# Tap products that write PSUM channel by channel, and copies out of PSUM that write SBUF at a step

## The chip, the cores and the metric

The kernel runs on one core of one Trainium2 chip. The metric is the time of one execution on the device in microseconds (us). TensorE is called PE, VectorE DVE, ScalarE ACT, GpSimd POOL; SP is the engine from whose queue most transfers are issued. A tile of PSUM holds 128 partitions; PSUM has eight banks of 512 fp32 numbers per partition, and the kernel hands them out as eight slots.

## The reference, cut to what matters

Two layers in a row over 2048 positions and 512 channels: a state-space convolution with a residual, and an MLP with a residual. The change lies in the making of the convolution kernel `K`, one row of 2048 taps for each of the 512 channels `d`, summed over 128 states `n`:

```python
dt = jnp.exp(log_dt)[:, None]
A = A_re + 1j * A_im
logdA = dt * A
dB = dt * Bc
P = jnp.exp(logdA[:, :, None] * l[None, None, :])
K = jnp.einsum("dn,dnl,dn->dl", Cc, P, dB).real
...
Yf = Uf * Kf[None, :, :, :]
y = irfft2(Yf)[..., :L] + u * Dskip
h = x + y
h2 = h + (gelu(layernorm(layernorm(h)) @ w1 + b1) @ w2 + b2)
```

## The kernel before, in words

**Stages.** The start loads the inputs and tables and prepares angles and magnitudes. Then exponentials and sines are made for the factors of `P` (up to about 105 us), with the first layer norm and the transform of the input between them. The taps are summed from the factors, transformed (`kspec`, `kspec1`, `fstage`), multiplied with the transform of the input (line 1203), transformed back (line 1213), and from about 145 us on the MLP runs (lines 1330 to 1348), with the second half of the convolution in between.

**The tap products.** A power of the state's factor is split in two: 20 offsets (the list `ROWS`, `NA` = 20) times 33 multiples of eight (`NB` = 33, from -16 to 16). For each channel the kernel holds a table of 128 states by 20 offsets and one of 128 states by 33 multiples, each as a real and an imaginary part: `EA`, `IA` and `EB`, `IB`. In SBUF the 128 channels of a group lie side by side within each offset, so one channel's 20 or 33 columns are 128 bf16 numbers (256 bytes) apart. A channel needs two matmuls, both over 128 states: real times real (line 1058) and imaginary times imaginary (line 1059), added up in PSUM. The weights are 128 by 20, the moving operand 128 by 33. There are four groups of 128 channels (`kgen(c)`, c = 0 to 3, called at lines 1373 and 1379), so 512 + 512 matmuls. Four channels, `g` = 0 to 3, go to the four column tiles of PE, each with its own 32 partitions of PSUM.

**The PSUM tile and the copy.** Within a group of 128 channels `i` counts the 32 channels of one column tile. They are filled in two tiles (`KIS`): one of two banks with 11 channels each, and one of a bank with 10. In a bank the sum for multiple `k` of channel `i` stands at place `k * n + i`, with `n` = 11 or 10: the channels are neighbours, and one matmul writes its 33 sums `n` numbers apart. When a tile is full, `evac` (lines 575 to 587) copies it to SBUF as bf16, on ACT (line 578) or DVE (line 580) as the written order says: 2 x 33 x 11 = 726 numbers a partition, or 33 x 10 = 330. In SBUF the place of a sum is `k` first and then the channel: `Kg` (groups 0 and 1 interleaved, 64 numbers from one `k` to the next) or `kgc` (groups 2 and 3, 32 numbers from one `k` to the next). So a copy writes runs of 11 or 10 neighbours, 128 or 64 bytes apart. Both copies of a group are followed by an addition on DVE at line 1072 (the skip term `Dz`), and then by the products that read the taps: line 1088 in `kspec` for groups 0 and 1, line 1113 in `kspec1` for groups 2 and 3, and line 1134 in `ktail`.

**Order.** The order of all operations is written out by hand in the list `ORDER`, which also says which of two engines takes a copy; the string `SLOTS` says which bank each PSUM tile gets. Each engine works through its own part in that order. The costs handed to `add` play no part at run time.

Of the kernel before, what the change touches and what calls it, by code (L numbers as in the profile page):

```python
# [25 lines left out]
NA = len(ROWS)  # L26
NB = 33
# [283 lines left out]
class Sched:  # L311
# [10 lines left out]
    def add(self, eng, cost, fn, r=(), w=(), new=(), lat=0.0, pr=None, byts=0, soft=(), softw=(), hv=None):  # L322
        o = Op()
        o.soft = sorted({self.wr[k] for x in soft for k in self.keys(x) if k in self.wr} | {i for x in softw for k in self.keys(x) for i in self.rd.get(k, ())})
        o.eng = eng if isinstance(eng, tuple) else (eng,)
        o.cost = cost if isinstance(cost, tuple) else (cost,)
        o.fn, o.lat, o.i, o.new, o.byts = fn, lat, len(self.ops), tuple(new), byts
        o.ni, o.act, o.st, o.md = 0, 0.0, 0.0, []
        o.hv = int(o.eng[0] == "DVE") if hv is None else hv
        o.pr = self.pr if pr is None else pr  # L330
        o.key = "%g%s" % (o.pr, o.eng[0][0])
        deps = set()
        for x in r:
            for k in self.keys(x):
                p = self.wr.get(k)
                if p is not None:
                    deps.add(p)
        for x in w:
            for k in self.keys(x):
                p = self.wr.get(k)  # L340
                if p is not None:
                    deps.add(p)
                deps.update(self.rd.get(k, ()))
        for x in r:
            for k in self.keys(x):
                self.rd.setdefault(k, []).append(o.i)
        for x in w:
            for k in self.keys(x):
                self.wr[k] = o.i
                self.rd[k] = []  # L350
        o.deps = sorted(deps)
        o.ps = [x for x in list(r) + list(w) if isinstance(x, Ps)]
        self.ops.append(o)
        return o
# [47 lines left out]
def c_dve(n, mode=1, psum=False):  # L402
    return (0.08 if n < 64 else 0.065) + n / mode / 960.0
# [3 lines left out]
def kernel(ctx, tc, A_u, A_A_re, A_A_im, A_B_re, A_B_im, A_C_re, A_C_im, A_log_dt, A_Dskip,  # L407
# [4 lines left out]
    class Pe:  # L412
        n, dry, act, st, md = 0, True, 0.0, 0.0, []
# [30 lines left out]
    def pst(p, dt=f32):  # L444
        a = banks[:, 512 * p.slot:512 * (p.slot + p.n)]
        return a if dt == f32 else a.bitcast(dt)
# [128 lines left out]
    def evac(out_fn, in_fn, n, r, w, pr=None, only=None):  # L575
        def fn(e):
            if e == "ACT":
                act.copy(out_fn(), in_fn())  # L578
            else:
                dve.tensor_copy(out_fn(), in_fn())  # L580
        if only == "ACT":
            add("ACT", c_act(n), fn, r=r, w=w, pr=pr)
        elif only == "DVE":
            add("DVE", c_dve(n, 1, True), fn, r=r, w=w, pr=pr, hv=0)
        else:
            add(("ACT", "DVE"), (c_act(n), c_dve(n, 1, True)), fn, r=r, w=w, pr=pr)
# [455 lines left out]
    def kgen(c, pr):  # L1042
        Ar, Br, Ai, Bi = EA[c], EB[c], IA[c], IB[c]
        kg = Kg[0] if c < 2 else kgc[c - 2]
        ks = (lambda: kg.ap()[:, :, c]) if c < 2 else kg.ap
        for grp in KIS:
            S.pr = pr + 0.01 * KIS.index(grp)
            p = Ps(n=len(grp))

            first = True  # L1050
            for nb, (i0, n) in enumerate(grp):
                for lo, hi in ((0, n // 2), (n // 2, n)):
                    def fn(e, p=p, nb=nb, i0=i0, n=n, lo=lo, hi=hi):
                        for i in range(lo, hi):
                            for g in range(4):
                                d = 32 * g + i0 + i
                                o = pst(p)[32 * g:32 * g + NA, 512 * nb:512 * nb + NB * n].rearrange("p (k i) -> p k i", i=n)[:, :, i]
                                pe.matmul(o, lhsT=Ar.ap()[:, :, d], rhs=Br.ap()[:, :, d], start=True, stop=False, tile_position=(0, 32 * g))  # L1058
                                pe.matmul(o, lhsT=Ai.ap()[:, :, d], rhs=Bi.ap()[:, :, d], start=False, stop=True, tile_position=(0, 32 * g))  # L1059
                    add("PE", 0.1376 * (hi - lo), fn, r=[Ar, Br, Ai, Bi], w=[p], new=[p] if first else [])  # L1060
                    first = False
            i0, n = grp[0]
            N = len(grp)

            def ofn(i0=i0, n=n, N=N):
                a = ks()[:, :, i0:i0 + n * N]
                return a.rearrange("p k (b i) -> p b k i", b=N)

            def ifn(p=p, n=n, N=N):
                return pst(p).rearrange("p (b q) -> p b q", b=N)[:, :, 0:NB * n].rearrange("p b (k i) -> p b k i", i=n)  # L1070
            evac(ofn, ifn, NB * n * N, [p], [kg])
        add("DVE", c_dve(32), lambda e: dve.tensor_tensor(ks()[:, 0], ks()[:, 0], Dz.ap()[:, c, :], ALU.add), r=[kg, Dz], w=[kg])

# [391 lines left out]
```

## Time and profile before

| | |
|---|---|
| median of 3 runs | 237.22 us (236.57 to 238.54) |
| the profiled execution, its own time | 235.58 us |
| its span, first to last instruction | 233.8 us |
| mean granted PE clock | 0.967 |
| PE busy | 204.2 us (87%) |
| DVE busy | 172.9 us (74%) |
| ACT busy | 158.6 us (68%) |
| lines 1058 and 1059 | 1024 matmuls between 58.0 and 104.9 us |
| copies out of the tap tiles | six on ACT, two on DVE, at 63, 71, 73, 74, 94, 94, 104 and 105 us |

How to read the lines that follow: a row of a group gives line, engine and operation, then what is written and read, partitions by elements, the count, the busy time in us, the mean duration of one in ns, and after the second bar the idle time of the engine before them with what ended it. `ar` is the one large SBUF tile in which everything lies, `ps` is PSUM, and `128*20 128x33` is a matmul with a weight of 128 by 20 and a moving operand of 128 by 33. PEld is the load of weights. A row in order of time gives the start in us, the duration in us, engine, line, operation and count. A row of the chain gives start and duration of one piece of the work that ended last. A row for one line gives durations as smallest, median and largest. Matmuls overlap one another, so their pace is seen in the distance of their starts.

### The profile page before, as it was taken

Reading aid. Unit: us, or ns where it says so; the run is one execution under the profiler, and the core shown is the slowest. Engines: PE = TensorE matmul, PEld = TensorE weight load, DVE = VectorE, ACT = ScalarE, POOL = GpSimd, SP = SyncE. Lnnn points to the kernel's source line nnn. Section 1 sums busy time; section 2 is a strip of 40 time slices with the busy share of each in tenths; the row PEclk is TensorE's granted clock in tenths of the full one; section 3 lists DMA queues with packets and bytes.
Section 4 is the critical chain, followed back from the end, with each engine's and each line's share of the span. In section 5 each row is a group of like instructions: output and inputs, shape, how many; then the busy total and the mean of one; then the engine's idle time right before and its main releaser. Section 6 shows DMA issues by size and latency. Waiting matters only on the chain.

```text
span 233.8 us, 8092 instructions
## 1 busy us (share of the span) xinstructions
PE 204.2 (87%) x3608; PEld 117.0 (50%) x3616; DVE 172.9 (74%) x282; ACT 158.6 (68%) x194; POOL 13.4 (6%) x23
## 2 busy tenths in 40 slices
PE   7318878888998996999999968999999999999992
PEld 4305633335675455677567555654444344444551
DVE  2999999999979765659799999989955993010222
ACT  4999999999986893756898479685155308405500
POOL 3000300000160000000000010100000110000000
PEclk9965999999999998899999999999999999999998
DMA  5998263270000363346989966530333045002212
GB/s 157 185 172 138 62 185 95 60 254 13 6 6 3 98 159 138 99 105 195 221 141 230 311 159 161 137 90 12 81 77 91 5 100 126 20 0 59 56 40 61
DMA packets 43160, 25.18 MB, mean 108 GB/s; under 512 B 30195, under 2 KB 40693, under 8 KB 43126
## 3 DMA queue, kind: packets, MB, share of 16 engines
q1 hardware_dynamic: 42142, 23.67, 41.9%
q10 hardware_dynamic: 984, 1.00, 1.4%
q8 instruction: 28, 0.46, 0.8%
q14 instruction: 6, 0.05, 0.1%
HBM read 14.14 MB, written 5.28 MB: 83 GB/s over the span
## 4 chain that ended last, share of the span: by engine, by line
PE 51%; DVE 15%; DMA 11%; ACT 11%; issue 5%; SPq 3%; POOL 2%; DVEq 0%; ACTq 0%
PE ps L1330 16%; PE ps L1346 16%; DMA ar<-in_A_u_dram 5%; ACT ar L578 4%; PE ps L1213 4%; ACT ar L1030 3%; SPq L594 3%; ACT ar L992 3%; PE ps L1058 3%; DVE ar L874 3%; DVE ar L1203 2%; PE ps L918 2%; PE ps L1028 2%; PE ps L1059 2%; DVE ar L922 2%
## 5 line engine op out<-in xcount | busy, mean ns | idle before, releaser
L578 ACT CAST ar<-ps 128x1024 bf16<-128x1024 f32 (+4 forms) x64 | 56.8, 940 | 14.9 <-PE ps L1213 4.1
L1332 ACT ACTIVATE ar<-ps,ar 128x512 bf16<-128x512 f32 (+1 forms) x44 | 27.8, 685 | 36.3 <-PE ps L1330 25.7
L1330 PE MATMUL ps<-ar 128*128 128x512 bf16 (+1 forms) x176 | 41.1, 379 | 0.0
L1346 PE MATMUL ps<-ar 128*128 128x512 bf16 (+2 forms) x180 | 40.2, 366 | 0.7 <-DVE ar L1290 0.2
L1348 DVE TENSOR_TENSOR ar<-ps,ar 128x512 bf16<-128x512 f32 (+1 forms) x17 | 10.7, 656 | 31.8 <-PE ps L1346 25.1
L580 DVE CAST ar<-ps 128x1024 bf16<-128x1024 f32 (+3 forms) x22 | 21.5, 988 | 9.6 <-PE ps L1059 2.9
L1346 PEld LDWEIGHTS <-ar 128*128 128x128 bf16 (+1 forms) x187 | 18.0, 98 | 20.1 <-issue 1.2
L1330 PEld LDWEIGHTS <-ar 128*128 128x128 bf16 (+1 forms) x176 | 17.2, 100 | 20.1 <-DMA ar<-in_B_w_dram 0.2
L1203 DVE TENSOR_TENSOR ar<-ar 128x2048 bf16<-128x2048 bf16 x20 | 23.8, 1218 | 0.6 <-PE ps L1213 0.5
L1030 ACT ACTIVATE ar<-ps 128x1024 bf16<-128x1024 int16 x20 | 19.9, 1039 | 5.0 <-PE ps L1028 4.4
L1213 PE MATMUL ps<-ar 64*128 64x128 bf16 x672 | 21.4, 216 | 1.7 <-DVE ar L1203 1.2
L1213 PEld LDWEIGHTS <-ar 64*128 64x128 bf16 x672 | 18.8, 94 | 6.2 <-issue 2.9
L1058 PE MATMUL ps<-ar 128*20 128x33 bf16 x512 | 20.1, 249 | 0.7 <-issue 0.7
L1059 PE MATMUL ps<-ar 128*20 128x33 bf16 x512 | 20.0, 247 | 0.0
L1058 PEld LDWEIGHTS <-ar 128*20 128x20 bf16 x512 | 16.8, 124 | 4.5 <-issue 4.1
L649 POOL TENSOR_TENSOR ar<-ar 128x4 f32<-128x4 f32 (+1 forms) x6 | 10.3, 1716 | 137.2 <-DVE ar L654 129.9
L897 PE MATMUL ps<-ar 128*32 128x512 bf16 x256 | 16.5, 381 | 1.5 <-ACT ar L957 1.2
L1059 PEld LDWEIGHTS <-ar 128*20 128x20 bf16 x512 | 17.3, 127 | 0.8 <-issue 0.4
L1028 PE MATMUL ps<-ar 128*32 128x256 f16 (+2 forms) x288 | 13.4, 289 | 3.6 <-issue 1.8
L992 ACT ACTIVATE ar<-ps 128x1024 bf16<-128x1024 int16 x16 | 15.8, 1050 | 0.8 <-PE ps L984 0.7
L744 ACT ACTIVATE ar<-ar 128x1024 bf16<-128x1024 f32 x16 | 15.6, 1047 | 0.6 <-DVE ar L1247 0.6
L918 PE MATMUL ps<-ar 128*64 128x512 bf16 (+2 forms) x160 | 14.7, 303 | 0.3 <-ACT ar L578 0.2
(87 smaller groups left out, 258.9 us busy)
## 6 DMA issues: line engine op xcount, KB each, us to landing
ar<-in_A_u_dram SPq DMA_DIRECT2D x16, 128.0 KB, 6.2
out_dram<-ar SPq DMA_DIRECT2D x30, 64.0 KB, 2.0
ar<-in_A_u_dram SPq DMA_DIRECT2D x7, 256.0 KB
ar<-in_B_w_dram SPq DMA_DIRECT2D x2, 640.0 KB, 6.2
ar<-in_B_w_dram SPq DMA_DIRECT2D x3, 344.0 KB, 7.6
AK_d<-ar SPq DMA_DIRECT2D x2, 512.0 KB, 4.2
ar<-AK_d SPq DMA_DIRECT2D x2, 512.0 KB
AKc_d<-ar SPq DMA_DIRECT2D x4, 256.0 KB, 4.5
```

The source lines that it names most:

```text
L578: act.copy(out_fn(), in_fn())
L580: dve.tensor_copy(out_fn(), in_fn())
L918: pe.matmul(pst(p)[64 * h:64 * h + 64, w * (k + r):w * (k + r) + w], lhsT=T.ap()[:, f, r, :], rhs=v[f:f + 1].ap()[:, 0, :], start=True, st ...
L992: add("ACT", c_act(1024), lambda e, p=p, sc=sc, cs=cs: act.activation(sc[cs].ap().rearrange("p c e d -> p e c d"), pst(p, i16).rearrange(" ...
L1030: add("ACT", c_act(1024), lambda e, sc=sc: act.activation(sc.ap().rearrange("p z a b -> p (z a b)"), pst(p, i16).rearrange("p (n two) -> p ...
L1058: pe.matmul(o, lhsT=Ar.ap()[:, :, d], rhs=Br.ap()[:, :, d], start=True, stop=False, tile_position=(0, 32 * g))
L1059: pe.matmul(o, lhsT=Ai.ap()[:, :, d], rhs=Bi.ap()[:, :, d], start=False, stop=True, tile_position=(0, 32 * g))
L1203: dve.tensor_tensor(pq.ap().rearrange("p n d -> p (n d)"), a, b_, ALU.mult)
L1213: pe.matmul(pst(p)[:, 512 * h + 128 * k:512 * h + 128 * k + 128], lhsT=q.ap()[rows, x, :], rhs=TP[w].ap()[rows, f0 // 2 + k, :], start=(n ...
L1330: pe.matmul(pst(p)[:fs], lhsT=w1s[dc].ap()[:, fc * P:fc * P + fs], rhs=ybuf.ap().rearrange("p (t c) k -> p c t k", c=4)[:, dc], start=(dc ...
L1332: add("ACT", c_act(512, 1), lambda e, p=p, fc=fc, fs=fs: act.activation(hT.ap()[:fs, fc, :], pst(p)[:fs], ACT.Gelu_apprx_tanh, bias=b1_sb. ...
L1346: pe.matmul(pst(p)[:, c0:c1], lhsT=hT.ap()[:fs, fc, 128 * t:128 * t + 128], rhs=w2s[fc].ap()[:fs, c0:c1], start=(fc == 0), stop=(fc == NFC ...
```

## The change

In the PSUM tile the two indices change places: the sum for multiple `k` of channel `i` now stands at `i * 33 + k`, so that a matmul writes 33 neighbours. The copy reads the tile in that order, straight through as before, and its output runs over `k` fastest: each bf16 number is written 64 numbers (`Kg`) or 32 numbers (`kgc`) after the one before. What lies where in SBUF after the copy is the same in both kernels. Numbers of instructions, engines, order, slots and transfers do not change.

```diff
                             for g in range(4):
                                 d = 32 * g + i0 + i
-                                o = pst(p)[32 * g:32 * g + NA, 512 * nb:512 * nb + NB * n].rearrange("p (k i) -> p k i", i=n)[:, :, i]
+                                o = pst(p)[32 * g:32 * g + NA, 512 * nb:512 * nb + NB * n].rearrange("p (i k) -> p i k", k=NB)[:, i, :]
                                 pe.matmul(o, lhsT=Ar.ap()[:, :, d], rhs=Br.ap()[:, :, d], start=True, stop=False, tile_position=(0, 32 * g))
                                 pe.matmul(o, lhsT=Ai.ap()[:, :, d], rhs=Bi.ap()[:, :, d], start=False, stop=True, tile_position=(0, 32 * g))
...
             def ofn(i0=i0, n=n, N=N):
                 a = ks()[:, :, i0:i0 + n * N]
-                return a.rearrange("p k (b i) -> p b k i", b=N)
+                return a.rearrange("p k (b i) -> p b i k", b=N)
 
             def ifn(p=p, n=n, N=N):
-                return pst(p).rearrange("p (b q) -> p b q", b=N)[:, :, 0:NB * n].rearrange("p b (k i) -> p b k i", i=n)
+                return pst(p).rearrange("p (b q) -> p b q", b=N)[:, :, 0:NB * n].rearrange("p b (i k) -> p b i k", k=NB)
             evac(ofn, ifn, NB * n * N, [p], [kg])
```

## The prediction

> **What bounds the kernel now.** I read the page first, then the groups by shape, then the order of time around the two places that the diff touches. On the page I took the busy shares, the slices, the chain's shares by line and the groups of the tap products:
>
> ```profile
> span 233.8 us, 8092 instructions
> PE 204.2 (87%) x3608; PEld 117.0 (50%) x3616; DVE 172.9 (74%) x282; ACT 158.6 (68%) x194; POOL 13.4 (6%) x23
> PE   7318878888998996999999968999999999999992
> ACT  4999999999986893756898479685155308405500
> PE ps L1330 16%; PE ps L1346 16%; DMA ar<-in_A_u_dram 5%; ACT ar L578 4%; PE ps L1213 4%; ACT ar L1030 3%; SPq L594 3%; ACT ar L992 3%; PE ps L1058 3%; DVE ar L874 3%; DVE ar L1203 2%; PE ps L918 2%; PE ps L1028 2%; PE ps L1059 2%; DVE ar L922 2%
> L1058 PE MATMUL ps<-ar 128*20 128x33 bf16 x512 | 20.1, 249 | 0.7 <-issue 0.7
> L1059 PE MATMUL ps<-ar 128*20 128x33 bf16 x512 | 20.0, 247 | 0.0
> ```
>
> PE is the engine that is nearly always busy, and it holds most of the chain that ended last. The two lines of tap products, 1058 and 1059, hold 3% and 2% of that chain, between 58 and 105 us. So there are two ways for this change to matter: through the pace of these 1024 matmuls, and through the eight copies out of their PSUM tiles.
>
> **The tap products.** Nothing is added or removed: still 512 + 512 matmuls, the same operands, the same order. Only the step of the PSUM writes goes from 11 (or 10) fp32 numbers to 1. What is this worth? Matmuls are pipelined, so I go by the starts and not by the means. Four of them (one for each column tile) form a packet:
>
> ```profile
> 57.98 0.27 PE L1058 MATMUL ps<-ar 128*20 128x33 bf16 x4
> 58.04 0.27 PE L1059 MATMUL ps<-ar 128*20 128x33 bf16 x4
> ...
> 58.59 0.26 PE L1059 MATMUL ps<-ar 128*20 128x33 bf16 x4
> ...
> 63.03 0.35 PE L1028 MATMUL ps<-ar 128*32 128x128 f16 x12
> 63.20 0.40 PE L1025 MATMUL ps<-ar 65*32 65x512 f16 x4
> ```
>
> From 57.98 to 58.59 lie nine packets: 68 ns each, for 33 columns, or 2.06 ns a column. The line-1028 group has the same four column tiles, straight reads and straight writes: three packets of 128 columns in 0.17 us, 57 ns each, 0.44 ns a column. So a tap packet pays almost five times the price per column. It differs in two ways: its outputs are stepped in PSUM, and both its operands are read at a step of 128 bf16 numbers in SBUF (one channel out of 128). The weight loads tell the two apart, since a load writes no PSUM:
>
> ```profile
> L984 PEld LDWEIGHTS <-ar x160: 88/88/90, 35.2 to 66.6; 64*32 64x32 f16 x160
> L1028 PEld LDWEIGHTS <-ar x288: 92/96/151, 47.6 to 94.2; 128*32 128x32 f16 x144
> L1287 PEld LDWEIGHTS <-ar x32: 106/106/110, 129.4 to 186.3; 128*64 128x64 bf16 x32
> L1058 PEld LDWEIGHTS <-ar x512: 111/123/145, 58.0 to 104.5; 128*20 128x20 bf16 x171
> ```
>
> Straight loads take 88 to 96 ns for 32 columns and 106 for 64, so 0.3 to 0.6 ns for each further column, and about 83 to 92 for 20. The stepped load of 20 columns takes 123, that is 31 to 40 ns too long, and 1.9 to 2.6 ns a column in all. The moving operand is read at the same step; at that price 33 columns take 63 to 86 ns, and the packet's 68 lie inside. The SBUF reads alone explain the pace, and they stay. I therefore take 0 for the matmuls. The bounds: no loss, since straight writes are what the 57-ns packets have; at most a gain down to 20 stepped weight columns, 20 x 2.06 = 41 ns a packet (rival C).
>
> [...]
>
> **The copies.** There are eight, two for each of four groups of channels: of 726 numbers a partition (four, all on ACT) and of 330 (two on ACT, two on DVE). Both kernels read PSUM straight. Writes went out in runs of 11 or 10 neighbours, and now every 2-byte number lands 128 bytes (first two groups) or 64 bytes (last two) from the one before. The rows:
>
> ```profile
> L578 ACT CAST ar<-ps 128x726 bf16<-128x726 f32 x4 | 3.1, 766 | 0.6 <-PE ps L1059 0.6
> L578 ACT CAST ar<-ps 128x330 bf16<-128x330 f32 x2 | 0.9, 441 | 0.0
> L580 DVE CAST ar<-ps 128x330 bf16<-128x330 f32 x2 | 1.0, 502 | 2.9 <-PE ps L1059 2.9
> L580 DVE CAST ar<-ps 128x1024 bf16<-128x1024 f32 x13 | 15.7, 1220 | 4.6 <-PE ps L918 2.3 <-PE ps L1155 1.0 <-PE ps L1088 0.7
> ```
>
> ACT: (766 - 441)/(726 - 330) = 0.82 ns a number and 170 fixed. DVE: (1220 - 502)/(1024 - 330) = 1.03 and 160 fixed. So runs of ten cost what a straight copy does; no row shows a write that steps at every number. Lower bound: 0.82 and 1.03, no change. Upper bound: the factor of PE's stepped against its straight columns, 2.06/0.44 = 4.7, or 3.9 ns on ACT and 4.8 on DVE. A gain is excluded, since the copies already run at the straight rate. I take PE's absolute price, 2.06 ns, as the nearest row: it is SBUF met at a 256-byte step, one number at a time. Then a 726 copy takes 170 + 726 x 2.06 = 1.67 us (+0.90), a 330 copy on ACT 0.85 (+0.41), on DVE 0.84 (+0.34). In sum 5.1 us of engine time; what of it is on the path I read off the order of time:
>
> ```profile
> 63.06 0.77 ACT L578 CAST ar<-ps 128x726 bf16<-128x726 f32 x1
> 69.93 1.04 ACT L1030 ACTIVATE ar<-ps 128x1024 bf16<-128x1024 int16 x1 [0.55 <-DVE ar L1004]
> 70.86 0.45 ACT L578 CAST ar<-ps 128x330 bf16<-128x330 f32 x1
> 73.47 0.77 ACT L578 CAST ar<-ps 128x726 bf16<-128x726 f32 x1 [0.40 <-PE ps L1059]
> 93.58 0.76 ACT L578 CAST ar<-ps 128x726 bf16<-128x726 f32 x1
> 104.26 1.11 ACT L578 CAST ar<-ps 128x726 bf16<-128x726 f32 x2 [0.15 <-PE ps L1059]
> ...
> 67.94 0.17 DVE L654 SCALAR_TENSOR_TENSOR ar<-ar 128x8 f32<-128x8 f32 x1 [1.43 <-POOL ar L649]
> 71.02 0.69 DVE L1034 TENSOR_TENSOR ar<-ar 128x1024 bf16<-128x1024 bf16 x1
> 73.45 0.68 DVE L1034 TENSOR_TENSOR ar<-ar 128x1024 bf16<-128x1024 bf16 x1
> 74.17 0.50 DVE L580 CAST ar<-ps 128x330 bf16<-128x330 f32 x1
> 94.71 0.17 DVE L1072 TENSOR_TENSOR ar<-ar 128x32 bf16<-128x32 bf16 x1
> 106.07 0.16 DVE L1072 TENSOR_TENSOR ar<-ar 128x32 bf16<-128x32 bf16 x1
> ```
>
> And the chain at the two places where a copy's result is waited for:
>
> ```profile
> 74.78 0.19 DVE ar L1072
> 75.01 1.91 PE ps L1088 x32
> ...
> 95.64 0.60 PE ps L1113 x16
> ...
> 106.42 0.60 PE ps L1113 x16
> ```
>
> - Groups 0 and 1 (63 to 75 us). Queued behind the copy at 63.06 on ACT are the sines and exponentials of lines 992, 884 and 1030. DVE waits 1.43 us for POOL there, which hides the +0.90 on DVE's side; ACT itself has 0.55 us of waiting before 69.93, so 0.35 is left. DVE's line 1034 at 71.02 starts as that activation ends, and DVE then works without a gap up to 74.17: its copy starts 0.35 late and lasts 0.34 longer. Line 1072 and the products of line 1088 wait for it: +0.7. The ACT copy of 73.47 would end at 75.14 and ask for less; the one of 70.86 vanishes in ACT's next wait.
> - Group 2 (93.58). The copy ends at 95.24 in place of 94.34. Line 1072 moves from 94.71 to 95.34 and ends at 95.5; PE turns to line 1113 only at 95.64. Hidden by the products of line 918: 0.
> - Group 3 (104.26). Both copies are on ACT: +1.31, so they end at 106.68. Line 1072, which DVE reaches at 106.07, waits until then, with line 922 behind it; line 1113 starts at 107.0 in place of 106.42: +0.6.
>
> Behind 106 us the chain goes on without slack (copies, the transfer out and back, then PE to the end), so I count these in full. Sum: 0 + 0.7 + 0 + 0.6 = +1.3 us. DMA issues, PSUM slots and the written order of the queues are unchanged. The profiled execution took 235.58 us (span 233.8 and 1.8 around it), which becomes 236.9. The median of the runs is 237.22, 1.64 above it, so the forecast is 238.5.
>
> **Rivals.** A is the sum above. B: the stepped write costs ACT and DVE more than PE's stepped read. At 2.5 ns the 726 copy takes 1.99 us (+1.2), the 330 ones +0.5; groups 0 and 1 give 0.65 + 0.5 = +1.15, group 2 ends at 95.85 (+0.2), group 3 +1.1: +2.5 us, 239.7. That is the point from which the change is slower by more than 1%. At the upper bound of 3.9 and 4.8 ns the three places give about +3, +1.3 and +2.6: 244. For it: these slots are the only cover, and the price is unknown. Against it: runs of ten cost nothing at all. [...]
>
> C: the PSUM step sets the pace of the taps after all. Their chain time is
>
> ```profile
> by line: PE ps L1058 9.7%; PE ps L918 8.2%; PE ps L1059 8.0%; PE ps L1028 7.1%; POOL ar L649 6.8%; PE ps L897 6.0%; issue 5.7%; DMA AKc_d<-ar 5.4%; DVE ar L1034 4.9%; ACT ar L1030 4.8%; PE ps L1088 4.5%; ACT ar L578 4.5%; DMA ar<-AKc_d 4.4%
> ```
>
> 17.7% of the 64 us from 56 to 120: 11.3 us. From 68 to 41 ns a packet this gives 11.3 x 27/68 = -4.5, and with the copies' +1.3 it ends at 234.0. A packet of 60 ns would already pay for the copies. For it: two steps are there and only one is measured apart. Against it: the loads above.
>
> D: a stepped write is free as well, and nothing changes: 237.2. [...]
>
> **How the numbers follow.** A 0.40, B 0.33, C 0.17, D 0.10. About 1% (2.4 us) is what a measurement of this kernel can tell from no change, as its three runs alone lie 2 us apart. Faster: C but for its weak end, 0.14. Slower: B, 0.33. The same: A, D and the rest of C, 0.53. A's own range is 237.5 to 239.6. The range of 8 in 10 goes from 235.5 (D with the scatter of the runs, and the weak end of C) to 241.5 (most of B); it leaves out some 0.12 of C and 0.08 of B.
>
> **What would show it.** In the changed profile: packets of lines 1058 and 1059 still 68 to 70 ns apart (A, B, D) or clearly less (C); the 726 rows of line 578 near 1.67 us (A), from 2.0 up (B) or still 0.77 (D); line 1088 some 0.7 us later after its last tap product, and line 1113 later behind 106 us, line 1113 near 95.6 not. The prediction is wrong if the packets get shorter, if stepped reads and stepped writes of SBUF have unlike prices, or if the late copies set free a stall elsewhere, such as ACT's next wait.

## The result, and the profile after

The changed kernel is slower: its median is 248.68 us over four runs (244.92 to 250.64), against 237.55 us for the kernel before on the same chip. The ratio is 1.036, with a 95% interval from 1.0245 to 1.0475; ratios leave out runs more than 1.5% above the fastest of the same kernel, here those of 250.07 and 250.64. Run again beside the experiments, the same kernel came out at 250.7 against 235.77 us, ratio 1.063 (1.0586 to 1.0673). The prediction had 238.5, with a range up to 241.5. The profiled execution took 247.28 us, span 245.5; for the kernel before these were 235.58 and 233.8. There are 11.7 us to be found.

The page of the changed kernel, the same parts as before, with one row added: PEclk, the clock granted to PE in each slice, in tenths of full speed:

```profile
span 245.5 us, 8092 instructions
PE 207.8 (85%) x3608; PEld 118.8 (48%) x3616; DVE 175.2 (71%) x282; ACT 171.0 (70%) x194; POOL 13.4 (5%) x23
PE   7419678979595999597799987999999999999992
PEclk9957999999859599799999999999999999999998
PE ps L1330 16%; PE ps L1346 16%; ACT ar L578 11%; DMA ar<-in_A_u_dram 5%; PE ps L1213 4%; ACT ar L992 4%; PE ps L1058 3%; SPq L594 3%; PE ps L1028 3%; PE ps L918 3%; PE ps L1059 2%; PE ps L897 2%; DVE ar L1203 2%; DVE ar L922 2%; PE ps L1088 2%
```

The number of instructions is the same. ACT is 12.4 us busier, and line 578, the copies, holds 11% of the chain in place of 4%. The clock row is the part that the prediction did not look at. Here is the same row of the kernel before:

```profile
PEclk9965999999999998899999999999999999999998
```

One slice is 5.8 us before and 6.1 us after. Behind the start, the kernel before lost a little clock in one place (slices 16 and 17, about 88 to 99 us); the changed kernel lost more, in three places (about 61 to 74, 80 to 86 and 98 to 104 us).

The groups by shape of the changed kernel, with the copies, the tap products and the products that read the taps:

```profile
L1058 PE MATMUL ps<-ar 128*20 128x33 bf16 x512 | 19.8, 248 | 3.1 <-ACT ar L578 2.5 <-issue 0.7
L578 ACT CAST ar<-ps 128x726 bf16<-128x726 f32 x4 | 13.6, 3389 | 0.6 <-PE ps L1059 0.6
L1088 PE MATMUL ps<-ar 20*128 20x512 bf16 x48 | 4.9, 574 | 2.5 <-DVE ar L1072 2.5
L578 ACT CAST ar<-ps 128x330 bf16<-128x330 f32 x2 | 3.6, 1782 | 0.6 <-PE ps L1059 0.6
L1113 PE MATMUL ps<-ar 20*128 20x256 bf16 x96 | 3.3, 269 | 4.3 <-DVE ar L1072 4.2
L580 DVE CAST ar<-ps 128x330 bf16<-128x330 f32 x2 | 3.2, 1621 | 2.6 <-PE ps L1059 2.6
L1072 DVE TENSOR_TENSOR ar<-ar 128x32 bf16<-128x32 bf16 x4 | 0.7, 176 | 7.4 <-ACT ar L578 7.4
```

The tap products (line 1058) are unchanged: 248 ns where they were 249. The copies are not. The large one takes 3389 ns in place of 766, the small ones 1782 and 1621 in place of 441 and 502. With the fixed times worked out before, 170 and 160 ns, the price of one stepped number is (3389 - 170)/726 = 4.43 ns on ACT and (1621 - 160)/330 = 4.43 ns on DVE. (The difference of the two sizes gives less on ACT, (3389 - 1782)/(726 - 330) = 4.06, but its two small copies took 1645 and 1918 ns, too far apart to be one price.) Follow the waits from the bottom: DVE's line 1072 waited 7.4 us for ACT's copies, and PE waited for line 1072, 2.5 us ahead of line 1088 and 4.2 ahead of line 1113. There is one wait more: the tap products themselves waited 2.5 us for a copy.

The order of time on PE of the changed kernel shows where:

```profile
58.08 0.27 PE L1058 MATMUL ps<-ar 128*20 128x33 bf16 x4
...
58.70 0.26 PE L1059 MATMUL ps<-ar 128*20 128x33 bf16 x4
...
66.68 0.27 PE L1058 MATMUL ps<-ar 128*20 128x33 bf16 x4 [2.46 <-ACT ar L578]
...
68.10 0.27 PE L1058 MATMUL ps<-ar 128*20 128x33 bf16 x4
...
68.84 0.26 PE L1059 MATMUL ps<-ar 128*20 128x33 bf16 x4
...
79.48 3.43 PE L1088 MATMUL ps<-ar 20*128 20x512 bf16 x32 [2.47 <-DVE ar L1072]
...
88.30 0.74 PE L1134 MATMUL ps<-ar 20*32 20x288 bf16 x32
...
104.27 0.62 PE L1113 MATMUL ps<-ar 20*128 20x256 bf16 x16 [1.29 <-DVE ar L1072]
...
118.37 0.62 PE L1113 MATMUL ps<-ar 20*128 20x256 bf16 x16 [2.87 <-DVE ar L1072]
```

And on ACT:

```profile
63.17 3.46 ACT L578 CAST ar<-ps 128x726 bf16<-128x726 f32 x1
...
73.39 6.68 ACT L578 CAST ar<-ps 128x330 bf16<-128x330 f32 x4 [0.59 <-PE ps L1059]
...
113.35 4.76 ACT L578 CAST ar<-ps 128x726 bf16<-128x726 f32 x2 [0.57 <-PE ps L1059]
```

The same PE rows of the kernel before:

```profile
64.03 0.27 PE L1058 MATMUL ps<-ar 128*20 128x33 bf16 x4
...
75.01 1.91 PE L1088 MATMUL ps<-ar 20*128 20x512 bf16 x32
...
80.80 0.68 PE L1134 MATMUL ps<-ar 20*32 20x288 bf16 x32
...
95.57 0.61 PE L1113 MATMUL ps<-ar 20*128 20x256 bf16 x16
...
106.35 0.61 PE L1113 MATMUL ps<-ar 20*128 20x256 bf16 x16
```

Set their starts side by side, and each step of the loss shows. Line 1088 started at 75.01 and now starts at 79.48: +4.5. Line 1134 started at 80.80, now 88.30: +7.5, so 3.0 more between them, though PE waits for nothing there. Line 1113 of group 2: 95.57 and 104.27, +8.7. Line 1113 of group 3: 106.35 and 118.37, +12.0. The end: +11.7. In steps: +4.5, +3.0, +1.2, +3.3 and -0.3.

What are the 3.0 us without a wait? The windows of the changed kernel answer (columns: stretch, length, busy time of PE, PEld, DVE, ACT, POOL, then the granted clock, the DMA share and GB/s):

```profile
66.10:72.90 6.80, 6.22 (x260) 4.63 (x263) 5.32 (x13) 6.70 (x8) 1.94 (x1) 0.50 0.02 5
79.50:86.50 7.00, 7.00 (x68) 2.48 (x71) 3.56 (x5) 3.46 (x4) 0.00 (x0) 0.52 0.22 67
100.20:103.60 3.40, 2.77 (x76) 1.47 (x67) 1.61 (x1) 3.40 (x3) 0.00 (x0) 0.50 0.25 80
```

About where each of the two 2.5-us waits ends (0.6 us before the end of the first, 0.2 us behind that of the second) the clock falls to a half, for 6.8 us. The 32 products of line 1088 take 3.43 us where they took 1.91. So PE seems to pay for its wait twice: while it waits, and again while it works at half clock. An experiment below tests this.

### The profile page after: what moved, and what is told of

Same layout as the page of the kernel before. It is cut to its first block, busy times and chain, and to the rows that moved or that the text cites. A ratio compares the mean times of both kernels' runs of the same rounds, so it can differ in the third digit from the quotient of the medians.

```text
span 245.5 us, 8092 instructions
## 1 busy us (share of the span) xinstructions
PE 207.8 (85%) x3608; PEld 118.8 (48%) x3616; DVE 175.2 (71%) x282; ACT 171.0 (70%) x194; POOL 13.4 (5%) x23
## 4 chain that ended last, share of the span: by engine, by line
PE 55%; ACT 17%; DVE 10%; DMA 8%; issue 5%; SPq 3%; DVEq 0%; ACTq 0%
PE ps L1330 16%; PE ps L1346 16%; ACT ar L578 11%; DMA ar<-in_A_u_dram 5%; PE ps L1213 4%; ACT ar L992 4%; PE ps L1058 3%; SPq L594 3%; PE ps L1028 3%; PE ps L918 3%; PE ps L1059 2%; PE ps L897 2%; DVE ar L1203 2%; DVE ar L922 2%; PE ps L1088 2%
## 5 line engine op out<-in xcount | busy, mean ns | idle before, releaser
L578 ACT CAST ar<-ps 128x1024 bf16<-128x1024 f32 (+4 forms) x64 | 69.1, 1155 | 15.8 <-PE ps L1213 4.0
L580 DVE CAST ar<-ps 128x1024 bf16<-128x1024 f32 (+3 forms) x22 | 23.7, 1090 | 11.3 <-PE ps L1088 4.0
L1030 ACT ACTIVATE ar<-ps 128x1024 bf16<-128x1024 int16 x20 | 20.3, 1057 | 3.4 <-PE ps L1028 3.3
L1058 PE MATMUL ps<-ar 128*20 128x33 bf16 x512 | 19.8, 248 | 3.1 <-ACT ar L578 2.5
L1059 PE MATMUL ps<-ar 128*20 128x33 bf16 x512 | 19.7, 247 | 0.0
L897 PE MATMUL ps<-ar 128*32 128x512 bf16 x256 | 17.3, 397 | 1.2 <-ACT ar L957 1.2
L1028 PE MATMUL ps<-ar 128*32 128x256 f16 (+2 forms) x288 | 14.1, 301 | 3.2 <-issue 1.7
L992 ACT ACTIVATE ar<-ps 128x1024 bf16<-128x1024 int16 x16 | 16.0, 1071 | 0.8 <-PE ps L984 0.8
```

Of the source, the lines that this page charges most:

```text
L897: pe.matmul(pst(p)[32 * j:32 * j + 32, 512 * z:512 * z + 512], lhsT=BX.ap()[:, f0 + z, 16 - 16 * c:48 - 16 * c], rhs=src[2 * j + c].ap(), ...
L992: add("ACT", c_act(1024), lambda e, p=p, sc=sc, cs=cs: act.activation(sc[cs].ap().rearrange("p c e d -> p e c d"), pst(p, i16).rearrange(" ...
```

## The experiments

**The two halves of the change.** The first kernel writes PSUM straight, as the change does, but its copies read PSUM at a step and write SBUF in runs as before. Against the changed kernel:

```diff
-                return a.rearrange("p k (b i) -> p b i k", b=N)
+                return a.rearrange("p k (b i) -> p b k i", b=N)
...
-                return pst(p).rearrange("p (b q) -> p b q", b=N)[:, :, 0:NB * n].rearrange("p b (i k) -> p b i k", k=NB)
+                return pst(p).rearrange("p (b q) -> p b q", b=N)[:, :, 0:NB * n].rearrange("p b (i k) -> p b k i", k=NB)
```

> The tap products write 33 neighbours in PSUM, as in the changed kernel; the copies read PSUM at a step of 33 fp32 numbers and write SBUF in runs of 11 or 10 as in the kernel before. Theory S (the whole loss is the stepped write to SBUF; the PSUM step neither costs nor gains): packets 69 ns apart, copies of 726 at 0.77 us, of 330 at 0.44 (ACT) and 0.50 (DVE), time within 1% of before, 236 to 239. Rival P (the copies are slow because of the new order on the PSUM side): copies of 726 above 2 us and more than half of the loss, over 243.

Measured: 235.9 against 235.4 us, ratio 1.0012 (0.9984 to 1.0041). Its copies, by shape:

```profile
L578 ACT CAST ar<-ps 128x726 bf16<-128x726 f32 x4 | 3.1, 767 | 0.7 <-PE ps L1059 0.6
```

The straight PSUM write brings nothing to the time, and a copy that reads PSUM 33 numbers apart costs what a straight one costs (767 and 766 ns).

The second kernel has the other half alone: PSUM stepped as before, SBUF written at a step. Against the kernel before:

```diff
-                return a.rearrange("p k (b i) -> p b k i", b=N)
+                return a.rearrange("p k (b i) -> p b i k", b=N)
...
-                return pst(p).rearrange("p (b q) -> p b q", b=N)[:, :, 0:NB * n].rearrange("p b (k i) -> p b k i", i=n)
+                return pst(p).rearrange("p (b q) -> p b q", b=N)[:, :, 0:NB * n].rearrange("p b (k i) -> p b i k", i=n)
```

> The tap products write PSUM at a step of 11 or 10 as in the kernel before; the copies write SBUF at a step as in the changed kernel, and so read PSUM at a step too. Theory S: copies of 726 at 3.3 to 3.5 us, of 330 at 1.6 to 1.9, the time of the changed kernel, 244 to 250. Rival P: copies near 0.8 us and a time within 1% of before.

Measured: 248.73 against 235.4, ratio 1.0572 (1.052 to 1.0623):

```profile
L578 ACT CAST ar<-ps 128x726 bf16<-128x726 f32 x4 | 13.5, 3386 | 0.0
```

The whole loss is in the copies' stepped writes.

**Which groups pay.** The changed layout for two of the four groups of channels only, the old one for the rest. The three lines of the change go under a condition:

```diff
+                return a.rearrange("p k (b i) -> p b i k" if c < 2 else "p k (b i) -> p b k i", b=N)
```

The second kernel has `c >= 2` in its place.

> The change made for channel groups 0 and 1 alone. Read off the two traces, line 1088 starts 4.5 us later there, and 3 us more follow until line 1134, while the granted clock is at half. Theory S with waits and clock: +6 to +8 us, 243 to 246, with a stretch at half clock near 80 us. Rival (waits at the four groups share one slack, so either half costs nearly all): +10 or more. Rival (the loss sits in groups 2 and 3): +3 or less.

> The change made for channel groups 2 and 3 alone. Read off the two traces: +1.5 us at line 1113 of group 2 and +2.9 at group 3. Theory S with waits: +3.5 to +5 us, 241 to 243, no new stretch at half clock before 90 us. Rival (one shared slack): +8 or more. Rival (groups 0 and 1 carry all): +1 or less.

Measured: groups 0 and 1 alone give 241.26, ratio 1.0257 (1.0213 to 1.0301); groups 2 and 3 alone 243.38, ratio 1.0331 (1.0285 to 1.0376). Their losses of 5.9 and 8.0 us add up to 13.8, near the 13.3 of all four in the kernel with the stepped write alone; with one shared slack each half would have cost nearly all of it. The first half came out just under what was expected, the half with groups 2 and 3 well above it. In its trace line 1113 of group 3 is late by 4.8 us (111.10 against 106.35), while its end is late by 6.7. Two windows of that kernel:

```profile
110.00:117.00 7.00, 5.90 (x124) 4.23 (x127) 4.69 (x8) 4.45 (x6) 0.00 (x0) 0.76 0.44 111
...
138.00:150.00 12.00, 9.35 (x190) 7.35 (x191) 11.22 (x21) 7.73 (x13) 1.01 (x1) 0.86 0.84 203
```

The clock is at 0.76 and 0.86 there; in the kernel before it is at 1.00 in the stretches that correspond to them (105.3 to 112.3 and 131 to 143 us). So a part of the loss comes behind the waits, and the clock is what the next kernels look at.

**Waits kept, half clock taken away.** If the 3.0 us behind line 1088 come from the clock, then PE kept busy during its wait should run line 1088 at full speed. Idle products, whose results nothing reads, go into the bank that line 1088 is about to overwrite (`fill`, four 128x128 matmuls each, line 1415), ahead of its first matmul:

```diff
+        first = next(o for o in order if o.fn.__name__ == "mm")
         for o in order:
+            if o is first:
+                for _ in range(11):
+                    fill(o.new[0].slot)
             o.fn(o.e)
```

> The changed kernel with eleven groups of four idle 128-column products on PE ahead of the first products of line 1088, into PSUM banks that these products use next; they fill the 2.5 us in which PE waits for the copies of groups 0 and 1. Theory K (the wait itself takes the granted clock to a half afterwards, and this costs 3 us): the clock stays at 1.0 after line 1088 starts, its 32 products take 1.9 us in place of 3.4, and the time is 2 to 3 us under the changed kernel's. Rival (line 1088 is slow for what it reads, or the clock falls for another reason): still 3.4 us, no gain, or a loss where the fill outlasts the wait.

Measured: 244.63 against 235.5, ratio 1.0348 (1.0261 to 1.0434). The same two windows of the changed kernel and then of this one:

```profile
75.90:79.50 3.60, 1.13 (x35) 0.53 (x26) 2.35 (x4) 3.60 (x3) 0.00 (x0) 1.00 0.00 0
79.50:83.00 3.50, 3.50 (x36) 1.41 (x39) 1.80 (x4) 0.60 (x2) 0.00 (x0) 0.53 0.02 5
```

```profile
75.90:79.50 3.60, 3.57 (x64) 2.84 (x65) 2.33 (x4) 3.60 (x2) 0.00 (x0) 1.00 0.02 5
79.50:83.00 3.50, 3.50 (x65) 1.47 (x68) 3.32 (x5) 2.11 (x3) 0.00 (x0) 1.00 0.00 0
```

Line 1088 starts at 79.48 in both: the wait is the same. But PE's 3.60 us ahead of it are full in place of 1.13, the clock stays at 1.00, and in the next 3.5 us 65 matmuls run in place of 36. Line 1134 starts at 85.3 in place of 88.3. This shows the 3.0 us, and the next kernel shows the same again. In the total the gain is not seen: the changed kernel was not timed beside this one, and this execution fell to half clock later (99.2 to 106 and 116.3 to 123.1 us), at waits that were not filled.

So the next kernel fills all three waits (11, 5 and 12 groups of four, ahead of line 1088 and of line 1113 in groups 2 and 3), timed beside the changed kernel itself on one chip (`new(n)` finds the operations that line `n` made, `age` the bank unused for longest):

```diff
+        want = dict(zip([new(1081)[0]] + new(1107), [11, 5, 12]))
         for t, o in enumerate(order):
+            if t in want:
...
+                for _ in range(want[t]):
+                    fill(min(age, key=age.get))
             o.fn(o.e)
```

> The changed kernel as it is, so that after_filled_all and after_in_pairs can be set beside it on one chip: 1.036 to 1.05 times the kernel before.

> The changed kernel with idle 128-column products on PE in three of its waits for copies: eleven groups of four ahead of line 1088, five ahead of the first products of group 2 at line 1113 and twelve ahead of those of group 3. after_filled moved the half clock from line 1088 to a place behind the third wait. Theory K (the waits themselves cost about 8 us, and the half clock that follows them about 3 us more): the half clock between 72 and 125 us goes, and the time falls by 2 to 4 us under after_same_chip, to 1.020 to 1.035 times the kernel before. Rival (the clock is no part of the loss, or moves on to a later place): within 1 us of after_same_chip.

Measured: the changed kernel 250.7 (ratio 1.0629, 1.0586 to 1.0673, above the 1.05 expected), the filled one 243.17 (ratio 1.0318, 1.0272 to 1.0363). The window from 72 to 125 us, changed kernel and then filled kernel:

```profile
72.00:125.00 53.00, 43.42 (x1220) 28.39 (x1213) 29.88 (x42) 37.67 (x33) 0.52 (x1) 0.82 0.31 88
```

```profile
72.00:125.00 53.00, 50.69 (x1513) 35.85 (x1503) 35.83 (x48) 43.93 (x42) 0.52 (x1) 1.00 0.41 113
```

With 112 useless matmuls more, the kernel is 7.5 us shorter, half of the 14.9 us that the change costs on this chip. That is more than was expected. The starts of the same rows tell where it comes from (us; the kernel before as in the trace above):

| | before | changed | filled |
|---|---|---|---|
| line 1088 | 75.01 | 80.03 | 79.89 |
| line 1134 | 80.80 | 88.44 | 85.68 |
| line 1113, group 2 | 95.57 | 104.87 | 99.91 |
| line 1113, group 3 | 106.35 | 119.15 | 114.03 |
| line 1134, second time | 111.50 | 127.32 | 119.18 |
| end of the span | 233.8 | 249.1 | 241.3 |

The filled kernel gains 2.6 us behind line 1088 and 3.0 behind line 1113 of group 3, where the changed kernel ran at half clock. The 2.2 us between line 1134 and group 2 are another matter. There the changed kernel has a stall that the profile calls "issue", as it shows nothing that PE waited for, with a stretch at half clock behind it:

```profile
99.84 0.41 PE L1028 MATMUL ps<-ar 128*32 128x256 f16 x4 [2.02 <-issue]
```

It is absent in the filled kernel; why, the runs do not tell. What the filled kernel still loses to the kernel before, 4.9 us by line 1088 and 3.3 between groups 2 and 3, are its waits for the copies.

**The tap products by themselves.** The prediction held that the stepped reads of SBUF set their pace and the PSUM step does not. Two kernels read both operands as neighbours; the second also writes PSUM straight:

```diff
-                                pe.matmul(o, lhsT=Ar.ap()[:, :, d], rhs=Br.ap()[:, :, d], start=True, stop=False, tile_position=(0, 32 * g))
+                                pe.matmul(o, lhsT=Ar.ap().rearrange("p a d -> p (a d)")[:, NA * d:NA * d + NA], rhs=Br.ap().rearrange("p a d -> p (a d)")[:, NB * d:NB * d + NB], start=True, stop=False, tile_position=(0, 32 * g))
```

> The kernel before, but each tap product reads 20 and 33 neighbouring bf16 numbers of its tables in place of numbers 256 bytes apart; the taps are then not the reference's, since other states' numbers are summed, while counts and sizes of all instructions stay. The PSUM writes keep their step of 11 or 10. Theory R (the stepped reads set the pace): packets of four fall from 69 ns to 20 to 40. Rival W (the stepped PSUM writes set it): they stay at 65 to 69.

> As reads_straight (taps not the reference's), with the 33 sums of a product side by side in PSUM as well. Theory R: packets as in reads_straight to 3 ns. Rival W2 (with straight reads the PSUM step becomes the limit): clearly shorter packets here than in reads_straight, 15 to 30 ns against 40 or more.

> The kernel of reads_straight again (taps not the reference's), now timed: its packets of tap products take 30 to 37 ns in place of 69, some 8 us of PE less, yet one look gave no shorter time. Theory (the taps' time on the chain is cover for ACT and DVE, which end up as the bound of that stage): within 1% of before. Rival (the share of the chain can be taken out as the prediction's rival C did): 4 us shorter or more, a ratio of 0.985 or less.

The order of time on PE, straight reads with the PSUM step (the timed run):

```profile
58.25 0.22 PE L1058 MATMUL ps<-ar 128*20 128x33 bf16 x4
...
58.47 0.21 PE L1059 MATMUL ps<-ar 128*20 128x33 bf16 x4
```

and straight in both:

```profile
58.89 0.20 PE L1058 MATMUL ps<-ar 128*20 128x33 bf16 x4
...
59.07 0.20 PE L1059 MATMUL ps<-ar 128*20 128x33 bf16 x4
```

Seven packets lie between the rows of each pair: 31 and 26 ns a packet, where stepped reads have 68. So the reads were worth 37 ns and the PSUM step 5, and those 5 only once the reads are out of the way. Yet the times are 236.16 and 238.07 us in single runs, and for the first kernel, timed twelve times, 235.6 against 235.77, ratio 1.0005 (0.9974 to 1.0036). Between 57 and 106 us PE is busy for 39.2 us in place of 45.6 in the timed run, and the kernel gains nothing. Its waits for ACT and DVE between 56 and 130 us grow from 1.1 to 5.5 us: in this stage these two stand close behind PE, and the taps are cover for them.

**The price of a stepped write.** Behind the end of the kernel before, copies of 320 fp32 numbers from PSUM, twice each, on ACT (lines 1440 to 1452) and then on DVE (1453 to 1465): bf16 at steps of 1, 2, 4, 8, 16, 32 and 64 numbers, bf16 in runs of 2, 4 and 8 every 64, fp32 at steps of 1, 2 and 32. In the edit `pr(s, r)` is a view of SBUF with runs of `r` numbers every `s`.

```diff
+        pr = lambda s, r=1: ar[:, 0:320 // r * s].rearrange("p (n s) -> p n s", s=s)[:, :, 0:r]
...
+            act.copy(pr(64)[:, :, 0], src)
...
+            act.copy(pr(64, 2), two(src, 2))
```

> The kernel before with copies added behind all its work: 320 fp32 numbers a partition from PSUM to SBUF on ACT and on DVE, the bf16 numbers 1, 2, 4, 8, 16, 32 or 64 places apart, in runs of 2, 4 or 8 every 128 bytes, and as fp32 numbers 1, 2 or 32 places apart. Theory G (the price is for each visit to another line of SBUF): singles rise with the step and level off near 4.1 ns on ACT and 4.4 on DVE from some step on, runs of 2 cost half as much per number, and fp32 numbers at the same byte step cost the same as bf16. Rival H (the price is for a write of two bytes alone): bf16 at a step of 2 costs as much as at 64, and runs of 2 and fp32 numbers at a step cost the straight price, 0.8 to 1.05 ns.

The run took 277.39 us with all of these copies. Their groups:

```profile
L1441 ACT CAST ar<-ps 128x320 bf16<-128x320 f32 x2 | 1.0, 514 | 0.1
L1442 ACT CAST ar<-ps 128x320 bf16<-128x320 f32 x2 | 1.7, 867 | 0.1
L1443 ACT CAST ar<-ps 128x320 bf16<-128x320 f32 x2 | 3.1, 1572 | 0.1
L1446 ACT CAST ar<-ps 128x320 bf16<-128x320 f32 x2 | 3.2, 1582 | 0.1
L1447 ACT CAST ar<-ps 128x320 bf16<-128x320 f32 x2 | 0.9, 428 | 0.1
L1451 ACT COPY ar<-ps 128x320 f32<-128x320 f32 x2 | 0.9, 440 | 0.1
L1452 ACT COPY ar<-ps 128x320 f32<-128x320 f32 x2 | 1.4, 692 | 0.1
L1459 DVE CAST ar<-ps 128x320 bf16<-128x320 f32 x2 | 3.2, 1580 | 0.1
```

A straight copy took 426 ns on ACT. Steps of 2, 4 and 8 numbers (4, 8 and 16 bytes) took 514, 867 and 1572; from there it is level to 6% up to 128 bytes (1582). Two neighbours every 128 bytes take 428: they are free. DVE has 1580 at the step where ACT has 1582, though its straight copy is slower (492): both engines come out at (1580 - 165)/320 = 4.4 ns a number there, with 165 for the fixed time. A copy of lone fp32 numbers 128 bytes apart takes 692, less than half of one of lone bf16 numbers. Neither theory came out whole: pairs are free, as H had it, but the price rises with the step up to 16 bytes, as G had it, and lone fp32 numbers lie between the two.

**A version that writes pairs.** If two neighbours are free, the taps can stay straight in PSUM and the copies can write two channels of one `k` at a time. The tiles then hold 12, 12 and 8 channels, all even:

```diff
-KIS = [[(0, 11), (11, 11)], [(22, 10)]]
+KIS = [[(0, 12), (12, 12)], [(24, 8)]]
...
-                return a.rearrange("p k (b i) -> p b i k", b=N)
+                return a.rearrange("p k (b i t) -> p b i k t", b=N, t=2)
...
-                return pst(p).rearrange("p (b q) -> p b q", b=N)[:, :, 0:NB * n].rearrange("p b (i k) -> p b i k", k=NB)
+                return pst(p).rearrange("p (b q) -> p b q", b=N)[:, :, 0:NB * n].rearrange("p b (i t k) -> p b i k t", k=NB, t=2)
```

> The changed kernel, with straight PSUM writes, in tiles of two banks of 12 channels and one of 8, whose copies write two channels' numbers side by side (one aligned word of four bytes) before they step on by 128 or 64 bytes. Theory H (only a lone two-byte write is dear): the copies, now of 792 and 264 numbers, take 0.82 and 0.39 on ACT and 0.43 on DVE, as in copies_probe for runs of two, and the time is within 1% of before. Rival G (each step to another line of SBUF is paid for): copies of 792 at 1.8 us or more, and a time 1 to 2% above before.

Measured: 233.72 against 235.77, ratio 0.9896 (0.9836 to 0.9956), about 1% under the kernel before. Its copies:

```profile
L578 ACT CAST ar<-ps 128x792 bf16<-128x792 f32 x4 | 3.5, 866 | 0.2 <-PE ps L1059 0.2
L580 DVE CAST ar<-ps 128x264 bf16<-128x264 f32 x2 | 0.9, 434 | 0.6 <-PE ps L1059 0.6
```

At the straight rate of 0.82 ns and 170 fixed, 792 numbers would take 819 ns; they take 866. The loss is gone. The gain over the kernel before is not in the copies, which are no cheaper. Up to line 1134 the two kernels run level (80.8 and 80.9 us); by line 1113 of group 2 the new one is 2.8 us ahead (92.8 against 95.57). Between the two lies this row of the kernel before, a stall that nothing in the trace explains:

```profile
92.13 0.40 PE L1028 MATMUL ps<-ar 128*32 128x256 f16 x4 [1.82 <-issue]
```

It is absent in the version with pairs, and so is the half clock that comes with it (91.9 to 95.3 us). That this is the gain is read off one trace of each kernel. The stall is also absent from the two filled kernels, whose taps are not in pairs, and stands with 1.6 to 3.2 us in all other traces here. Why, was not tried, so whether the 1% belongs to the layout stays open.

## Why the prediction was wrong, point by point

**Right: the tap products cost 0.** From 58.08 to 58.70 in the changed kernel lie nine packets, 69 ns each; the half of the change with straight PSUM alone came out at 1.0012. The SBUF reads set the pace (31 ns a packet with straight reads and the PSUM step kept), as the weight loads had told.

**Rightly given a small chance, but wrong in its price as well: rival C.** Even if the packets had got shorter, as C had it, the 4.5 us would not have come: packets of 31 ns gave a ratio of 1.0005. C took the taps' share of the chain for something that can be saved. The share said only that PE was the last to end at those moments; ACT and DVE stood close behind.

**Wrong, and the step that decided: "I take PE's absolute price, 2.06 ns, as the nearest row".** A stepped bf16 write costs 4.43 ns on ACT and on DVE. The large copy was to take 1.67 us and took 3.39. PE's stepped read and these engines' stepped write both touch SBUF one number at a time, but that did not make them one price, as the prediction's own list of signs had allowed for. The upper bound in the text, 3.9 and 4.8, was right in size, and its 244 was left out of the range, though the only row held against it, the runs of ten, has no write that steps at every number. No run shows the 2.5 ns from which rival B's 239.7 is worked out: the stepped write took 4.43, and the time came out at 248.68. It was not the price of every lone number either: an fp32 number by itself, 32 numbers from the next, took (692 - 170)/320 = 1.63 ns on ACT in the probe.

**Right in place, short in size: where the copies are waited for.** The text named line 1088 and line 1113 of group 3, and for the upper bound group 2 as well, with +3, +2.6 and +1.3. These came out as +4.5, +3.3 and +1.2. Groups 0 and 1 were short because one consumer was left out: the PSUM tile itself. The copy at 63.17 lasts 3.46 us; the next tap tile gets the same two banks (by the string `SLOTS`), so its first product starts only at 66.68, after a wait of 2.46. Even the +0.90 that the prediction took would have been felt there: the copy would have ended at 64.73, and that product started at 64.03 in the kernel before. So the small copy behind it starts at 73.39 in place of 70.86, 2.5 late. From there to the end of the large copy ACT took 3.38 us before, with 1.14 of waiting in it (0.74 and 0.40), and now takes 5.84 without a wait. The large copy ends 5.0 us late, of which 0.5 go into line 1072's slack. The prediction asked who waits for the result of a copy, and not who waits for its source.

**Missing: the clock.** No term said that a wait of PE is paid again. The 3.0 us behind line 1088 are shown by the filled kernel. With all three waits filled half of the loss went, 5.6 us of it from stretches at half clock behind the waits and 2.2 with the stall. Without this term, and without the PSUM tile, the upper bound of the price still gave 244, short of the median of 248.68.

**Right: the reading of PSUM.** Copies that read it straight or 33 numbers apart take 766 and 767 ns.

## What to carry to other kernels

When a layout is turned around, look at which side of the copy the step lands on: a step on the PSUM side was free or 5 ns a packet here, and lone 2-byte writes to SBUF 16 to 128 bytes apart cost four to five times a straight write, number for number (4.1 to 4.4 ns against 0.82 on ACT and 1.03 on DVE), while pairs every 128 bytes cost nothing on ACT (428 against 426 ns a copy). When a producer gets slower, follow both ends of it, who waits for its result and who waits for the buffer that it empties. Price a wait of PE of about two microseconds above its own length, since the matmuls behind it may run at half clock (stalls and waits of 1.7 to 2.9 us were followed by a granted clock of 0.50 here in some executions, and the one of 2.47 cost 3.0 us more that way); where no row shows a price, keep the upper bound in the range.

## What the runs showed of the hardware

- A lone bf16 number cost ACT and DVE the same, 4.1 to 4.4 ns (copies of 1492 to 1582 ns), at steps of 16 to 128 bytes. At 8 bytes it cost (867 - 170)/320 = 2.2: that copy took twice the straight time of 426 ns.
- Waits of PE of 2.46 and 2.47 us each led into 6.8 us at a granted clock of 0.50, and a stall of 1.82 (in the kernel before) into 3.4 us. Not every such wait is: behind the one of 2.87 us at 118.37 the clock stayed at 1.00, while in the second run of the same kernel the stretch from 120.1 to 126.9 was at half. Which wait brings it varies from run to run, and the spread of the changed kernel's times may come from that: over its ten runs the mean granted clock falls from 0.946 at 244.92 us to 0.920 at 251.03. This was not tried.
- Tap packets with stepped reads keep their pace at half clock. From 68.10 to 68.84, in the window at 0.50, lie eleven packets of 67 ns. At a clock of 1.00 they took 69, so their limit here is not the clock of PE.
